# Converting float64 weights a whole unit at a time on VectorE and ScalarE alone, with the words loaded into the unit's own place

## The chip, the cores and the metric

One core of one Trainium2 chip runs the kernel. The metric is device microseconds (us) of one execution; before the change the median of 3 runs is 819.43 us (818.68 to 821.88).

## The reference, cut to what matters

Three layers follow one another: retention over 4 x 8 heads of 576 tokens, a dense layer of 2304 tokens x 512 x 2048 with a gated activation, and eight experts of which each token takes one. The dense layer's weights come to the kernel as float64, since they are drawn as float32 and multiplied by a float64 scalar.

```python
ret = scores * Dmat[None, :, :, :]
attn_out = np.matmul(ret, v)                      # (4, 8, 576, 64) -> x: (2304, 512)
...
h = x @ w_in                                      # float64 weights, 512 x 2048
g = h * (1.0 / (1.0 + np.exp(-1.702 * h)))
x = g @ w_out                                     # float64 weights, 2048 x 512
...
expert_idx = np.argmax(logits, axis=1)
out[mask] = gate_w[mask, None] * (np.maximum(x[mask] @ w1[e], 0.0) @ w2[e])
```

## The kernel before, in words

**Units.** The dense layer's 2048 hidden columns fall into 16 units of 128 (NF1). A unit holds, for each of 128 partitions, 512 numbers of w_in and 512 of w_out, in two float32 parts: a high part that TensorE multiplies in one pass, and a low part, which is the rest. So a unit is a tile of 128 x 2 x 1024. Sixteen such places form a ring (tag "unit"); the retention stage uses seven of them first, for its own tables (`slot`, L178).

**Conversion.** The float64 words come as pairs of 32-bit words (`load_wd`, L113, by SP's queue). `convert` (L119) makes a float32 of each pair: ScalarE (ACT) takes the magnitude of the high word (L121), VectorE (DVE) clamps it (L137, a tensor_scalar), shifts and masks it (L143, a tensor_scalar), puts sign and top exponent bit back (L147, a scalar_tensor_tensor), and brings in three bits of the low word (L151, likewise). Then ACT writes the high part (L127, a CAST) and GpSimd (POOL) subtracts it to get the low part (L128). All of this is done by halves of a unit, 512 numbers a partition, so that each of these lines runs 32 times. `convert` is a generator: it yields an estimate of its cost, and `pull(us)` (L648) takes pieces out of it until `us` are used up. Retention's last 24 steps each pull 0.4, and each step of the dense layer's first two blocks pulls 2.5.

**The dense layer.** Tokens fall into six blocks of 384. Blocks 0 and 1 go through the 16 units side by side (steps g0 to g31: unit 0 for block 0, unit 0 for block 1, unit 1 for block 0, and so on), and the other four blocks follow one by one (steps g32 to g95). A step i is `layer1`, 12 matmuls into h (L374); `swish`, which is a tanh on ACT (L396), a scalar_tensor_tensor on DVE (L398), a CAST on ACT that makes the high part of g (L399), and a subtraction that makes the low part (L400: on POOL for the first three blocks, where `early` is set, on DVE after them); and two steps later `layer2`, nine matmuls into o (L385). h has two buffers, so the matmuls of step i+2 wait until L398 of step i has read h. Every engine takes its instructions in the order in which this code issues them.

**Around it.** Retention's step (bp, ch) is a chunk of one pair of heads; 16 pairs (bp) of 5 chunks each. Tables and inputs of pair bp+3 are loaded at the end of pair bp, into three sets of buffers (kz, at). The same SP queue issues the words of the weights: four half units at pairs 3, 4, 7 and 9 (WD_AT, L43), the others from within `convert`, two units ahead of their use; these wait for their staging buffers (tags "stg" and "tab"). It also writes back the retention's result for blocks 2 to 5 (x0d, L314).

The functions that the change touches:

Of the kernel before, what the change touches and what calls it, by code (L numbers as in the profile page):

```python
# [10 lines left out]
F32 = mybir.dt.float32  # L11
F32R = mybir.dt.float32r
BF16 = mybir.dt.bfloat16
I32 = mybir.dt.int32
AF = mybir.ActivationFunctionType
ALU = mybir.AluOpType

P = 128
# [7 lines left out]
NF1 = F1 // P  # L26
# [13 lines left out]
WARM = 34  # L40
HOLD = NF1 - LAG - 1 - KD
STOP = 1000.0
WD_AT = (3, 4, 7, 9)  # L43
CLAMP_HI = float(np.array(0x47EFFFFF, np.int32).view(np.float32))


# [13 lines left out]
def retention_moe_kernel(  # L60
# [40 lines left out]

    units = {}

    def new_unit(u):
        units[u] = pool.tile([P, 2, 1024], F32R, tag="unit", bufs=NF1, name=f"unit{u}")
        return units[u]

    stg = {}

    ca = pool.tile([P, 4, 512], I32, tag="tab", bufs=2, name="ca")  # L110
    cs = pool.tile([P, 2, 1024], I32, tag="tab", bufs=2, name="cs")

    def load_wd(i):  # L113
        u, h = divmod(i, 2)
        t = cs[:, h, :] if u % 2 else pool.tile([P, 1024], I32, tag="stg", bufs=2, name=f"wd{i}")
        stg["d", i] = t.rearrange("p (n two) -> p n two", two=2)
        SP.dma_start(t, wd[u, :, 512 * h : 512 * (h + 1)].bitcast(I32))

    def convert():  # L119
        def magnitude(i):  # L120
            ACT.activation(ca[:, i % 4, :].bitcast(F32), stg["d", i][:, :, 1].bitcast(F32), AF.Abs)  # L121

        def split(i):
            u, h = divmod(i, 2)
            f = ca[:, i % 4, :].bitcast(F32)
            hi, lo = (units[u][:, k, 512 * h : 512 * (h + 1)] for k in range(2))
            ACT.copy(hi, f)  # L127
            POOL.tensor_tensor(lo, f, hi.bitcast(F32), ALU.subtract)  # L128

        for i in range(2):  # L130
            magnitude(i)
        for u in range(NF1):
            new_unit(u)
            halves = [2 * u, 2 * u + 1]
            for i in halves:
                a = ca[:, i % 4, :].bitcast(F32)
                DVE.tensor_scalar(a, a, 2.0**-15, CLAMP_HI, ALU.max, ALU.min)  # L137
                if u:
                    split(i - 2)
                yield 0.35  # L140
            for i in halves:
                a = ca[:, i % 4, :]
                DVE.tensor_scalar(a, a, 3, 0x3FFFFFF8, ALU.logical_shift_left, ALU.bitwise_and)  # L143
                yield 0.35
            for i in halves:
                a = ca[:, i % 4, :]
                DVE.scalar_tensor_tensor(a, stg["d", i][:, :, 1], -0x40000000, a, ALU.bitwise_and, ALU.bitwise_or)  # L147
                yield 0.61
            for i in halves:
                a = ca[:, i % 4, :]  # L150
                DVE.scalar_tensor_tensor(a, stg.pop(("d", i))[:, :, 0], 29, a, ALU.logical_shift_right, ALU.bitwise_or)  # L151
                if u + 2 < NF1:
                    load_wd(i + 4)
                if u + 1 < NF1:
                    magnitude(i + 2)
                yield 0.61
        for i in halves:
            split(i)
            yield 0.1

    def load_we(u):
        t = pool.tile([P, 1024], F32, tag="stg", bufs=2, name=f"we{u}")
# [13 lines left out]
    st = {}  # L176

    def slot(name):  # L178
        return pool.tile([P, 2048], F32, tag="unit", bufs=NF1, name=name)

    def attention():
        psum = tc.tile_pool(name="psum_a", bufs=1, space=bass.MemoryType.PSUM, reuse_waits="tile")
# [206 lines left out]
    def swish(h, name, early=False, kept=None):  # L389
        th = pool.tile([P, TB], F32, tag="th", bufs=2, name=f"{name}t")  # L390
        if kept:
            hi, lo = kept
        else:
            hi = pool.tile([P, TB], F32R, tag="g", bufs=6, name=f"{name}h")
            lo = pool.tile([P, TB], F32R, tag="g", bufs=6, name=f"{name}l")
        ACT.activation(th, h, AF.Tanh, scale=0.851)  # L396
        g = th if early else h
        DVE.scalar_tensor_tensor(g, th, 1.0, h, ALU.add, ALU.mult)  # L398
        ACT.copy(hi, g)  # L399
        (POOL if early else DVE).tensor_tensor(lo, g, hi.bitcast(F32), ALU.subtract)  # L400
        return hi, lo

    def relu(h, name):
# [205 lines left out]
    def overflow_expert(e):  # L609
# [4 lines left out]
        DVE.scalar_tensor_tensor(ids, sel, -BIG, big, ALU.mult, ALU.add)  # L614
        w = []
        for k in range(NF2 // 2):
            t = pool.tile([P, 2, 1024], F32, tag="unit", bufs=NF1, name=f"vw{e}_{k}")
            for j in range(2):
                SP.dma_start(t[:, j, :], we[NF2 * e + 2 * k + j])
                w.append(t[:, j, :])  # L620
# [27 lines left out]
    def pull(us):  # L648

        k = 0  # L650
        us += debt.pop()
        while us > 0 and k < len(bg):
            cost = next(bg[k], None)
            if cost is None:
                bg.pop(k)
            elif cost == STOP:
                k += 1
                us -= 0.7
            else:
                us -= cost  # L660
        debt.append(min(us, 0.0))

    bg.append(convert())
    for i, _ in enumerate(attention()):
        if i > 55:
            pull(0.4)
    psum = ctx.enter_context(tc.tile_pool(name="psum", bufs=1, space=bass.MemoryType.PSUM, reuse_waits="tile"))

    def fill_slots():
# [140 lines left out]
    for i in range(nd - 1):  # L810
        blk, f = steps[i]
        dense1(i)
        if blk < 2:
            pull(2.5)
            if f > 3:
                next(fill, None)
            if (blk, f) == (1, NF1 - 3):
# [148 lines left out]
```

## Time and profile before

| | |
|---|---|
| median of 3 runs | 819.43 us (818.68 to 821.88) |
| the profiled execution | 821.95 us, span 820.2 us |
| busy, share of the span | PE 93%, DVE 56%, ACT 41%, POOL 39% |
| 105 to 212 us of the span | DVE 102.68 of 107.00 us busy, PE 94.90 |
| instructions, DVE / ACT / POOL | 982 / 700 / 292 |

The profile is of one execution. PE is TensorE, PEld its weight loads, SPq the queue that issues transfers. Busy time of PE is modelled and can hide that it is not at its peak. A row of the instruction list has the start in us of the span, the duration in us, the engine, the line of the code, the operation and its tiles (out<-in), and in brackets how long the engine sat idle before it and what ended that. A row with x2 or x12 stands for that many instructions, and its duration runs from the first one's start to the last one's end. The profiled execution was 2.52 us above the median of the runs.

### The profile page before, as it was taken

The page shows a single profiled execution, that of the slowest core. Times are in us where ns is not written, and L with a number is a line of the kernel's source. Part 1 is how long each engine was busy: PE and PEld are TensorE (multiplying, and loading weights), DVE is VectorE, ACT ScalarE, POOL GpSimd, SP SyncE. Part 2 cuts the span into 40 slices and gives each one's busy share as a digit, 9 for nine tenths or more (in the row PEclk, how much of TensorE's full clock was granted, in tenths as well). Part 3 has the DMA queues.
Part 4 walks back from the last instruction along what each step waited for, and adds up shares of the span by engine and source line. Part 5 has one row for each costly group of instructions (what it writes and reads, how often), then busy time and mean ns, then how long its engine had stood idle before and what let it go on. Part 6 is the DMA issues. An engine that isn't in the chain of part 4 may idle for free.

```text
span 820.2 us, 13383 instructions
## 1 busy us (share of the span) xinstructions
PE 765.9 (93%) x4996; PEld 674.2 (82%) x4996; DVE 462.6 (56%) x982; ACT 337.8 (41%) x700; POOL 319.8 (39%) x292
## 2 busy tenths in 40 slices
PE   7786798889999999999999998999999999999995
PEld 6666687777898989898999997888888888888884
DVE  4443789999414978774475388573434434354310
ACT  3665744444345332332332333334535434444321
POOL 3433566666623453111011122333545545454311
PEclk9998999999999999999999999999999999999998
DMA  8788833568601021203000333434536646456200
GB/s 275 239 287 261 254 131 119 161 180 256 222 1 40 2 65 52 78 1 103 14 0 21 109 103 103 148 116 149 173 142 178 184 135 192 143 182 190 79 30 34
DMA packets 37130, 105.64 MB, mean 129 GB/s; under 512 B 5439, under 2 KB 8895, under 8 KB 36800
## 3 DMA queue, kind: packets, MB, share of 16 engines
q1 hardware_dynamic: 33824, 95.24, 36.8%
q0 software_dynamic: 3232, 9.46, 3.1%
q8 instruction: 41, 0.67, 0.3%
q14 instruction: 33, 0.27, 0.1%
HBM read 81.55 MB, written 24.18 MB: 129 GB/s over the span
## 4 chain that ended last, share of the span: by engine, by line
PE 49%; issue 6%; DVE 5%; POOL 2%; ACT 1%; DMA 1%; POOLq 0%; ACTq 0%
PE eo L385 12%; PE o L385 12%; PE eh L374 12%; PE h L374 11%; DVE dj L468 2%; PE tp L573 1%; DMA we<-we 1%; DVE unit L170 1%; POOL out L412 1%; POOL unit L171 1%; DVE h L398 1%; ACT unit L169 0%; PE tp L743 0%; PE dots L482 0%; PE tp L748 0%
## 5 line engine op out<-in xcount | busy, mean ns | idle before, releaser
L374 PE MATMUL h<-x,unit 128*128 128x384 f32 x1152 | 219.3, 338 | 14.3 <-DVE x_k L400 2.5
L374 PEld LDWEIGHTS h<-x,unit 128*128 128x128 f32 x1152 | 202.6, 188 | 29.6 <-DVE x_k L400 3.8
L171 POOL TENSOR_TENSOR unit<-we,unit 128x512 fp32r<-128x512 f32 x64 | 105.0, 1649 | 149.3 <-ACT unit L169 144.7
L374 PE MATMUL eh<-xt,unit 128*128 128x352 f32 x672 | 117.1, 323 | 0.0
L374 PEld LDWEIGHTS eh<-xt,unit 128*128 128x128 f32 x672 | 111.0, 188 | 6.3
L468 DVE CUSTOM_DVE_ANT_0 dj<-xr,en 128x512 f32<-128x512 f32 x120 | 101.2, 896 | 2.2 <-ACT xr L452 2.2
L170 DVE TENSOR_TENSOR unit<-we,unit 128x512 fp32r<-128x512 f32 x64 | 58.4, 912 | 43.3 <-ACT unit L169 43.3
L169 ACT CAST unit<-we 128x1024 fp32r<-128x1024 f32 x64 | 66.8, 1046 | 9.1 <-DMA we<-we 9.1
L271 ACT ACTIVATE at<-kv,tb 64x64 f32<-64x64 f32 x128 | 39.5, 308 | 28.5 <-PE kv L268 19.7
L128 POOL TENSOR_TENSOR unit<-ca,unit 128x512 fp32r<-128x512 f32 x32 | 47.5, 1501 | 4.1 <-ACT unit L127 3.9
L240 DVE TENSOR_TENSOR pr<-sc,tb 128x256 f32<-128x256 f32 x64 | 26.7, 422 | 34.7 <-PE sc L239 31.8
L239 PE MATMUL sc<-at,kz 128*64 128x128 f32 (+1 forms) x512 | 36.0, 262 | 10.3 <-DMA at<-att 8.7
L412 POOL DMA_INDIRECT out<-y,idx x24 | 23.6, 983 | 49.2 <-ACT y L582 45.3
L239 PEld LDWEIGHTS sc<-at,kz 128*64 128x64 f32 x512 | 29.9, 148 | 11.4 <-issue 5.4
L252 POOL TENSOR_TENSOR kz<-at,tb 128x512 f32<-128x512 f32 x15 | 15.6, 1042 | 58.6 <-DMA at<-att 42.0
L268 PE MATMUL kv<-at,kz 128*64 128x64 f32 x256 | 21.8, 248 | 14.2 <-ACT at L271 12.4
L268 PEld LDWEIGHTS kv<-at,kz 128*64 128x64 f32 x256 | 13.7, 142 | 25.1 <-ACT at L271 22.9
L412 POOL DMA_INDIRECT xs<-xr,slot x18 | 19.1, 1061 | 27.6 <-DVE ov_all L547 23.6
L143 DVE TENSOR_SCALAR ca<-ca 128x512 int32<-128x512 int32 x32 | 28.2, 910 | 0.0
L289 PE MATMUL ao<-pr,at 128*64 128x128 f32 x256 | 26.6, 284 | 0.0
L367 POOL TENSOR_TENSOR x<-x0s,x 128x768 fp32r<-128x768 f32 x3 | 6.3, 2086 | 49.8 <-ACT x L366 49.8
L137 DVE TENSOR_SCALAR ca<-ca 128x512 f32<-128x512 f32 x32 | 22.8, 730 | 3.2 <-ACT ca L121 3.1
(1266 smaller groups left out, 1566.9 us busy)
## 6 DMA issues: line engine op xcount, KB each, us to landing
we<-we SPq DMA_DIRECT2D x64, 512.0 KB, 3.4
at<-att SPq DMA_DIRECT2D x15, 864.0 KB, 5.5
wd<-wd SPq DMA_DIRECT2D x16, 512.0 KB, 3.8
cs<-wd SPq DMA_DIRECT2D x16, 512.0 KB, 5.1
xs<-fill SPq DMA_DIRECT2D x22, 257.0 KB, 5.5
xrow<-xr SPq DMA_DIRECT2D x18, 257.0 KB, 5.1
kz<-kt SPq DMA_DIRECT2D x32, 144.0 KB, 4.0
rin<-xs SPq DMA_DIRECT2D x8, 514.0 KB, 4.4
```

Of the source, the lines that this page charges most:

```text
L128: POOL.tensor_tensor(lo, f, hi.bitcast(F32), ALU.subtract)
L143: DVE.tensor_scalar(a, a, 3, 0x3FFFFFF8, ALU.logical_shift_left, ALU.bitwise_and)
L169: ACT.copy(w[:, 0, :], t)
L170: DVE.tensor_tensor(w[:, 1, :512], t[:, :512], w[:, 0, :512].bitcast(F32), ALU.subtract)
L171: POOL.tensor_tensor(w[:, 1, 512:], t[:, 512:], w[:, 0, 512:].bitcast(F32), ALU.subtract)
L239: PE.matmul(sc[64 * i : 64 * i + 64, j, q0:], z[:, k0 : k0 + 64], t[:, AQ + P * ch + q0 : AQ + P * (ch + 1)], start=True, stop=True)
L268: PE.matmul(kv[r], z[:, 2 * S + P * ch + 64 * j : 2 * S + P * ch + 64 * j + 64], t[:, AV + P * ch + 64 * j : AV + P * ch + 64 * j + 64], s ...
L271: ACT.activation(sbd[(NCH * bp + ch) % 3][r, r], kv[r], AF.Copy, scale=tb[r, pair, TDW + P + 2 * NCH + ch : TDW + P + 2 * NCH + ch + 1])
L374: PE.matmul(h, w[:, a, P * dc : P * (dc + 1)], xt[:, b, dc, :n], start=k == 0, stop=k == len(terms) - 1)
L385: PE.matmul(o, a[:, c0 : c0 + n], w[:, b, 512:], start=first and k == 0, stop=last and k == 2)
L412: i = POOL.indirect_dma_start(out=dst[:, :], out_offset=bass.IndirectOffsetOnAxis(ap=rows, axis=0), in_=src, in_offset=None, bounds_check= ...
L468: DVE.tensor_tensor_reduce(junk, r[:, :D], en[e // 4][:, e % 4, :], 1.0, 0.0, ALU.mult, ALU.add, dots[:, E * k + e : E * k + e + 1])
```

## The change

Each conversion step now takes a whole unit, 1024 numbers a partition. The words of unit u are loaded by one transfer of 1 MB into the place in the ring that unit u itself will take; the working copy (`words`, two buffers) has the staging buffers. The place is now a fixed number, HELD + u modulo 16. Words are loaded three units ahead: units 0, 1 and 2 at retention's pairs 4, 7 and 10, unit u+3 when the last word operation of unit u has been issued. The low part of a unit is subtracted on DVE, after the second operation of the next unit. Also the low part of g is subtracted on DVE for all blocks. Retention's last 24 steps pull 0.5, and the steps of blocks 0 and 1 pull 3.1. The lines of the changed kernel are up to four lower than those before: its L126 is the magnitude, L134 and L136 the two tensor_scalar, L142 and L146 the two scalar_tensor_tensor, L150 ACT's CAST, L129 the low part of the unit, L392, L394, L395 and L396 the four parts of swish.

```diff
-WD_AT = (3, 4, 7, 9)
+WD_AT = (4, 7, 10)
+NWD = len(WD_AT)
+HELD = 7
...
+    def unit_tile(name, shape, dt, s):
+        return pool.tile(shape, dt, tag=f"unit{s % NF1}", bufs=1, name=name)
+
     def new_unit(u):
-        units[u] = pool.tile([P, 2, 1024], F32R, tag="unit", bufs=NF1, name=f"unit{u}")
+        units[u] = unit_tile(f"unit{u}", [P, 2, 1024], F32R, HELD + u)
         return units[u]
...
-    def load_wd(i):
-        u, h = divmod(i, 2)
-        t = cs[:, h, :] if u % 2 else pool.tile([P, 1024], I32, tag="stg", bufs=2, name=f"wd{i}")
-        stg["d", i] = t.rearrange("p (n two) -> p n two", two=2)
-        SP.dma_start(t, wd[u, :, 512 * h : 512 * (h + 1)].bitcast(I32))
+    def load_wd(u):
+        t = unit_tile(f"wd{u}", [P, 2048], I32, HELD + u)
+        stg["d", u] = t.rearrange("p (n two) -> p n two", two=2)
+        SP.dma_start(t, wd[u].bitcast(I32))
...
+        words = [pool.tile([P, 1024], I32, tag="stg", bufs=2, name=f"ca{k}") for k in range(2)]
+
+        def magnitude(u):
+            ACT.activation(words[u % 2].bitcast(F32), stg["d", u][:, :, 1].bitcast(F32), AF.Abs)
+
+        def low(u):
+            DVE.tensor_tensor(units[u][:, 1, :], words[u % 2].bitcast(F32), units[u][:, 0, :].bitcast(F32), ALU.subtract)
+
+        magnitude(0)
         for u in range(NF1):
+            a = words[u % 2]
+            DVE.tensor_scalar(a.bitcast(F32), a.bitcast(F32), 2.0**-15, CLAMP_HI, ALU.max, ALU.min)
+            yield 0.67
+            DVE.tensor_scalar(a, a, 3, 0x3FFFFFF8, ALU.logical_shift_left, ALU.bitwise_and)
+            yield 0.67
+            if u:
+                low(u - 1)
+                yield 1.22
+            d = stg.pop(("d", u))
+            DVE.scalar_tensor_tensor(a, d[:, :, 1], -0x40000000, a, ALU.bitwise_and, ALU.bitwise_or)
+            if u + 1 < NF1:
+                magnitude(u + 1)
+            yield 1.22
+            DVE.scalar_tensor_tensor(a, d[:, :, 0], 29, a, ALU.logical_shift_right, ALU.bitwise_or)
+            if u + NWD < NF1:
+                load_wd(u + NWD)
             new_unit(u)
...
+            ACT.copy(units[u][:, 0, :], a.bitcast(F32))
+            yield 1.22
+        low(u)
+        yield 0.1
...
-        (POOL if early else DVE).tensor_tensor(lo, g, hi.bitcast(F32), ALU.subtract)
+        DVE.tensor_tensor(lo, g, hi.bitcast(F32), ALU.subtract)
...
         if i > 55:
-            pull(0.4)
+            pull(0.5)
...
         if blk < 2:
-            pull(2.5)
+            pull(3.1)
```

What this does to the order of instructions is shown at three places. The first is DVE from step g6 to step g8 of the dense layer. Before, ca is the working copy and wd or cs the words:

```order
L398 SCALAR_TENSOR_TENSOR g6t<-g6t,h_1690 128x384
L147 SCALAR_TENSOR_TENSOR ca<-wd_1590,ca 128x512
L151 SCALAR_TENSOR_TENSOR ca<-wd_1586,ca 128x512
L151 SCALAR_TENSOR_TENSOR ca<-wd_1590,ca 128x512
L137 TENSOR_SCALAR ca<-ca 128x512
L398 SCALAR_TENSOR_TENSOR g7t<-g7t,h_1732 128x384
L137 TENSOR_SCALAR ca<-ca 128x512
L143 TENSOR_SCALAR ca<-ca 128x512 x2
L147 SCALAR_TENSOR_TENSOR ca<-cs,ca 128x512 x2
L151 SCALAR_TENSOR_TENSOR ca<-cs,ca 128x512
L398 SCALAR_TENSOR_TENSOR g8t<-g8t,h_1771 128x384
```

And DVE with the change, at the same steps:

```order
L394 SCALAR_TENSOR_TENSOR g6t<-g6t,h_1637 128x384
L396 TENSOR_TENSOR g6l<-g6t,g6h 128x384
L142 SCALAR_TENSOR_TENSOR ca_1076<-wd_1488,ca_1076 128x1024
L146 SCALAR_TENSOR_TENSOR ca_1076<-wd_1488,ca_1076 128x1024
L394 SCALAR_TENSOR_TENSOR g7t<-g7t,h_1673 128x384
L396 TENSOR_TENSOR g7l<-g7t,g7h 128x384
L134 TENSOR_SCALAR ca_1077<-ca_1077 128x1024
L136 TENSOR_SCALAR ca_1077<-ca_1077 128x1024
L129 TENSOR_TENSOR unit_1662<-ca_1076,unit_1662 128x1024
L142 SCALAR_TENSOR_TENSOR ca_1077<-wd_1550,ca_1077 128x1024
L394 SCALAR_TENSOR_TENSOR g8t<-g8t,h_1707 128x384
```

Two subtractions that were POOL's, L396 and L129, now stand among DVE's, and the operations of one unit follow one another without another half between them. The second place is ACT at the same steps, before:

```order
L399 CAST g6h<-g6t 128x384
L121 ACTIVATE ca<-cs 128x512 x2
L127 CAST unit_1671<-ca 128x512
L396 ACTIVATE g7t<-h_1732 128x384
L399 CAST g7h<-g7t 128x384
L127 CAST unit_1671<-ca 128x512
L121 ACTIVATE ca<-wd_1712 128x512
L396 ACTIVATE g8t<-h_1771 128x384
```

and with the change:

```order
L395 CAST g6h<-g6t 128x384
L126 ACTIVATE ca_1077<-wd_1550 128x1024
L150 CAST unit_1662<-ca_1076 128x1024
L392 ACTIVATE g7t<-h_1673 128x384
L395 CAST g7h<-g7t 128x384
L126 ACTIVATE ca_1076<-wd_1621 128x1024
L392 ACTIVATE g8t<-h_1707 128x384
```

The CAST of a whole unit (L150) now stands right ahead of the tanh of a step (L392), and it needs the operation L146 that stands right ahead of that step's L394 on DVE. The third place is SP's queue between the inputs of pairs 9 and 10 (at and kz), before:

```order
L198 DMA at_86<-att 128x1728
L117 DMA cs<-wd 128x1024
L314 DMA x0d_62<-xf_786 128x384
L196 DMA kz_84<-kt 64x576 x2
L198 DMA at_87<-att 128x1728
```

and with the change:

```order
L194 DMA at_84<-att 128x1728
L119 DMA wd_769<-wd 128x2048
L310 DMA x0d_62<-xf_783 128x384
L192 DMA kz_82<-kt 64x576 x2
L194 DMA at_85<-att 128x1728
```

A transfer of 1 MB (wd, 128x2048 words) stands ahead of the inputs of pair 10 where half of it stood. The next one, unit 2, is issued behind the inputs of pair 12, where before a half was issued behind those of pair 11; the one after it, unit 3, stands behind the inputs of pair 14, where before a half stood. PE's order is the same in both kernels.

## Rows read from the trace of the kernel before

**Rows 1.** The page: the span.
```profile
span 820.2 us, 13383 instructions
```

**Rows 2.** Windows: the stretch, busy us by engine, clock, DMA share, GB/s.
```profile
60.00:105.00 45.00, 32.83 (x588) 27.78 (x586) 26.32 (x55) 28.49 (x86) 20.58 (x22) 0.92 0.79 252
105.00:212.00 107.00, 94.90 (x457) 80.57 (x457) 102.68 (x129) 49.59 (x99) 70.34 (x50) 1.00 0.55 170
```

**Rows 3.** The chain that ended last: start, us, what.
```profile
340.46 2.08 PE o L385 x9
342.54 2.10 PE h L374 x12
```

**Rows 4.** The line L398: durations in ns, then first and last start.
```profile
L398 DVE SCALAR_TENSOR_TENSOR g11t<-g11t,h x1: 541/541/541, 164.2 to 164.2; 128x384 f32<-128x384 f32 x1
```

**Rows 5.** Instructions in order of time, DVE, 204 to 222 us.
```profile
203.99 0.54 DVE L398 SCALAR_TENSOR_TENSOR g19t<-g19t,h 128x384 f32<-128x384 f32 x1
204.45 0.75 DVE L137 TENSOR_SCALAR ca<-ca 128x512 f32<-128x512 f32 x2
205.12 0.75 DVE L143 TENSOR_SCALAR ca<-ca 128x512 int32<-128x512 int32 x2
...
206.54 0.55 DVE L398 SCALAR_TENSOR_TENSOR g20t<-g20t,h 128x384 f32<-128x384 f32 x1
...
221.24 0.55 DVE L398 SCALAR_TENSOR_TENSOR g24t<-g24t,h 128x384 f32<-128x384 f32 x1 [3.63 <-ACT g24t L396]
```

**Rows 6.** Groups by line and shape: busy us, mean ns, idle before.
```profile
L143 DVE TENSOR_SCALAR ca<-ca 128x512 int32<-128x512 int32 x32 | 28.2, 910 | 0.0
```

**Rows 7.** Instructions in order of time, POOL, 118 to 124 us.
```profile
119.83 2.90 POOL L128 TENSOR_TENSOR unit<-ca,unit 128x512 fp32r<-128x512 f32 x2
```

**Rows 8.** Instructions in order of time, DVE, 118 to 125 us.
```profile
120.08 2.94 DVE L143 TENSOR_SCALAR ca<-ca 128x512 int32<-128x512 int32 x2
122.94 0.68 DVE L147 SCALAR_TENSOR_TENSOR ca<-wd,ca 128x512 int32<-128x512 int32 x1
123.54 0.54 DVE L398 SCALAR_TENSOR_TENSOR g3t<-g3t,h 128x384 f32<-128x384 f32 x1
```

**Rows 9.** Instructions in order of time, DVE, 345 to 347 us (block 3).
```profile
345.27 0.56 DVE L398 SCALAR_TENSOR_TENSOR h<-g53t,h 128x384 f32<-128x384 f32 x1 [0.56 <-ACT g53t L396]
346.38 0.56 DVE L400 TENSOR_TENSOR g53l<-h,g53h 128x384 fp32r<-128x384 f32 x1 [0.55 <-ACT g53h L399]
346.85 0.69 DVE L468 CUSTOM_DVE_ANT_0 dj<-xr,en 128x512 f32<-128x512 f32 x1
```

**Rows 10.** Instructions in order of time, ACT, 200 to 207 us.
```profile
200.31 1.23 ACT L121 ACTIVATE ca<-cs 128x512 f32<-128x512 f32 x2
201.46 0.47 ACT L396 ACTIVATE g19t<-h 128x384 f32<-128x384 f32 x1
...
204.98 1.14 ACT L127 CAST unit<-ca 128x512 fp32r<-128x512 f32 x2
206.02 0.48 ACT L396 ACTIVATE g20t<-h 128x384 f32<-128x384 f32 x1
```

**Rows 11.** Instructions in order of time, PE in retention, with their waits.
```profile
65.33 0.56 PE L239 MATMUL sc<-at,kz 128*64 128x128 f32 x8 [2.79 <-DMA at<-att]
...
78.86 0.56 PE L239 MATMUL sc<-at,kz 128*64 128x128 f32 x8 [2.52 <-DMA at<-att]
```

**Rows 12.** Instructions in order of time, PE at pair 15.
```profile
97.88 0.56 PE L239 MATMUL sc<-at,kz 128*64 128x128 f32 x8 [2.21 <-DMA at<-att]
```

**Rows 13.** Instructions in order of time, SP's queue: transfers issued.
```profile
52.17 0.42 SPq L117 DMA_DIRECT2D cs<-wd  x1
...
56.91 0.51 SPq L198 DMA_DIRECT2D at<-att  x1
...
65.21 0.34 SPq L117 DMA_DIRECT2D cs<-wd  x1
```

**Rows 14.** Instructions in order of time, PE in block 2.
```profile
293.87 0.17 PE L515 MATMUL rk<-oh_all,ub 128*128 128x24 bf16 x1 [1.71 <-DVE dots L468]
```

More of the change, by code (lines that the diff above doesn't have):

```diff
@@ L102, in retention_moe_kernel @@
     units = {}
+    def unit_tile(name, shape, dt, s):
+        return pool.tile(shape, dt, tag=f"unit{s % NF1}", bufs=1, name=name)
     def new_unit(u):
-        units[u] = pool.tile([P, 2, 1024], F32R, tag="unit", bufs=NF1, name=f"unit{u}")
+        units[u] = unit_tile(f"unit{u}", [P, 2, 1024], F32R, HELD + u)
         return units[u]
     stg = {}
-    ca = pool.tile([P, 4, 512], I32, tag="tab", bufs=2, name="ca")
-    cs = pool.tile([P, 2, 1024], I32, tag="tab", bufs=2, name="cs")
-    def load_wd(i):
-        u, h = divmod(i, 2)
-        t = cs[:, h, :] if u % 2 else pool.tile([P, 1024], I32, tag="stg", bufs=2, name=f"wd{i}")
-        stg["d", i] = t.rearrange("p (n two) -> p n two", two=2)
-        SP.dma_start(t, wd[u, :, 512 * h : 512 * (h + 1)].bitcast(I32))
@@ L119, in convert @@
-    def convert():
[L120 to L131, printed above, removed]
-        for u in range(NF1):
-            new_unit(u)
[L134 to L159, printed above, removed]
@@ L178, in slot @@
     def slot(name):
-        return pool.tile([P, 2048], F32, tag="unit", bufs=NF1, name=name)
+        st["slots"] = st.get("slots", -1) + 1
+        assert st["slots"] < HELD
+        return unit_tile(name, [P, 2048], F32, st["slots"])
     def attention():
@@ L616, in overflow_expert @@
         for k in range(NF2 // 2):
-            t = pool.tile([P, 2, 1024], F32, tag="unit", bufs=NF1, name=f"vw{e}_{k}")
+            t = unit_tile(f"vw{e}_{k}", [P, 2, 1024], F32, k)
             for j in range(2):
```

## The prediction

> **What bounds the kernel now.** I read the windows first, then the chain of waits, then the instructions in order of time on the engine that the chain blames. The profiled execution took 821.95 us, of which the span is 820.2 us [rows 1]. In a dense step without waiting PE works 2.10 us on the 12 matmuls into h and 2.08 us on the nine into o, so 4.18 us a step [rows 3]. One stretch is far from that: from 105 to 212 us DVE is busy for 102.68 of 107.00 us, PE for 94.90 [rows 2]. That is where the weights are converted. There the step's scalar_tensor_tensor on DVE, which frees h, starts at 123.54 us for g3, 164.2 us for g11 and 203.99 us for g19 [rows 4, 5, 8]: 40.7 and 39.8 us for eight steps, **5.03 us a step**. DVE sets the pace there. By g24, at 221.24 us, the conversion is over and PE sets it [rows 5].
>
> Why DVE is so slow there is seen at 120 us. Two tensor_scalar take 2.94 us while two of POOL's subtractions run, which take 2.90 us [rows 7, 8]; with POOL idle the same pair is started and followed within 0.67 us [rows 5]. So POOL's work costs DVE time, and over the kernel the 32 of L143 alone took 28.2 us, 910 ns each [rows 6], where 0.67/2 x 32 is 10.7 us.
>
> **The change part by part.** With POOL's subtractions gone from this stretch, DVE runs at the undisturbed rate. I price a whole unit's operations from undisturbed halves. A scalar_tensor_tensor over 512 is followed 0.60 us after its start [rows 8], one over 384 after 0.46 us [rows 5]. That is 1.0 to 1.1 ns a number (the rows are rounded) and some 0.06 us for the start, which a whole saves once: 1.14 us over 1024 (bounds 1.09 and 1.20). A tensor_scalar is 0.67 us for two halves [rows 5], so 0.61 us (bounds 0.56 and 0.67). No row has the subtraction over 1024; like the scalar_tensor_tensor it reads two tensors, so I take 1.14 us for it as well. A unit is then 2 x 0.61 + 3 x 1.14 = 4.64 us of DVE.
>
> The Trainium skill, page "SBUF — State Buffer", section "Who interferes with whom", says that a VectorE instruction with two SBUF inputs, or in a two-port mode, and a GpSimd instruction that reads SBUF exclude one another for the whole instruction. The trace agrees for the tensor_scalar [rows 7, 8]. By that rule alone the conversion would be all gain, the first rival below.
>
> The subtraction of g's low part comes on top. In block 3, where it already is DVE's, scalar_tensor_tensor, wait for ACT's CAST and subtraction together take DVE from 345.27 to 346.85 us: 1.58 us a step, of which 0.55 us is idle [rows 9]. Before, DVE spent 0.46 us a step on this [rows 5]. The pattern of the order repeats after eight steps: 8 x 3.1 of pull against 2 x 0.67 + 3 x 1.22 = 5.0 a unit is five units. So DVE's own sum for eight steps is 5 x 4.64 + 8 x 1.58 = **35.8 us**, 4.48 us a step. That is less than 5.03, but already more than PE's 4.18.
>
> Now the wait that the order adds. ACT's CAST of a whole unit stands right ahead of a step's tanh, and it needs the last word operation on DVE. Behind that operation DVE has the step's scalar_tensor_tensor, which needs the tanh. So DVE stands idle for CAST and tanh together, although h has long been ready, and PE waits behind it. A CAST of two halves takes ACT 1.04 us from start to the next start [rows 10]; I take 1.0 us for a whole. The magnitude takes 1.15 us for two halves [rows 10]; I take 1.1 us. From the tanh's start to DVE's it is 0.52 us (206.02 to 206.54 us) [rows 5, 10]. Counted over the eight steps g2 to g9 of the changed order, what stands ahead of the step's scalar_tensor_tensor on DVE is
>
> - the last word operation, twice: 1.0 + 0.52 = 1.52 us idle each, 3.0 us;
> - the first tensor_scalar of the next unit, once: 1.52 - 0.61 = 0.9 us;
> - the second tensor_scalar, once: 1.52 - 1.22 = 0.3 us;
> - the sign operation, twice: the next unit's magnitude starts with it, so 1.1 + 0.52 - 1.14 = 0.5 us each, 1.0 us;
> - the unit's subtraction, twice: nothing.
>
> Together 5.2 us. Also, an operation that needs the result of the one right before it can't start in its tail, which is 0.08 us (0.68 us long, followed after 0.60 us) [rows 8]; eight such places make 0.6 us. So eight steps take 35.8 + 5.2 + 0.6 = 41.6 us: **5.2 us a step**, against 5.03 before. And conversion now lasts until g22 in the order.
>
> From g3, which I leave at 123.5 us, to g22 are 19 steps: 123.5 + 19 x 5.2 = 222.3 us. g22 frees h 0.55 us later, PE then needs 2.10 us for the matmuls of g24, and the tanh 0.52 us: g24 on DVE at 225.5 us, where it was 221.24 us [rows 5]. **The dense stretch loses 4.3 us.** After that PE sets the pace as before, so nothing gives them back. Bounds: without the idle time 4.48 us a step and a gain of 9.4 us (the first rival); with the upper prices of all operations about 5.4 us a step and a loss of 8 us.
>
> Retention pulls its inputs through a busy SP queue. The DMA share there is 0.79 at 252 GB/s [rows 2], and PE waits at three places for inputs that came late: 2.79, 2.52 and 2.21 us [rows 11, 12]. Half a unit is 0.52 MB: 1.6 us at a full share (252/0.79 = 319 GB/s), 2.1 us at 252. Unit 1 now puts 1 MB ahead of pair 10's inputs, where half of it was issued at 52.17 us, before the inputs at 56.91 us that came at 65.33 us [rows 11, 13]: + 1.6 to 2.1 us on the first wait. The half at 65.21 us [rows 13] no longer stands ahead of pair 12's inputs: as much less on the second. Unit 3 stands ahead of pair 15's with 1 MB where half stood: 0 to + 2.1 us. I take + 1.0 us in all, between - 2.2 us (the third wait goes, since no load waits for its staging buffer any longer) and + 4.2 us. Retention's DVE has room for its part of the conversion (26.32 of 45.00 us) [rows 2]: nothing.
>
> In block 2 the low part of g moves onto DVE beside the routing. There PE waited once, 1.71 us [rows 14], on DVE's dot products. These are no longer held up by POOL, but each step has 1.1 us more in front of them. I take nothing, bounds - 1.7 and + 1.5 us. The other edits (places in the ring, names) issue nothing.
>
> Sum: 4.3 + 1.0 + 0 = + 5.3 us, 827.3 us on the profiled execution. That one lay 2.52 us above the median of the runs shown, so against the median: 819.43 + 5.3 = **824.7 us**.
>
> **Rivals.** *VectorE freed and ACT in time: faster.* If the tanh were ready when DVE comes to it, eight steps would be DVE's own 35.8 us, g22 would be at 123.5 + 19 x 4.48 = 208.6 us, and g24 at 211.8 us: 9.4 us earlier, with + 1.0 us in retention 811.0 us. For it: POOL's price in rows 6 to 8 is real and goes. Against it: the order printed above puts the CAST ahead of the tanh. It decides as soon as the idle time falls below 2 us in eight steps. The rule of the Trainium skill on the shared ports, taken alone, gives this time.
>
> *The words flood retention's queue: slower still.* If the DMA share is full from 50 to 100 us, units 1, 2 and 3 delay inputs by 2.1 us each and nothing is given back: + 6.3 us there in place of + 1.0, 830.0 us. For it: three late inputs already. Against it: a mean share of 0.79 leaves 9 of the 45 us free.
>
> *Both prices cancel: no change.* With half of the idle time (2.6 us) a step takes 4.88 us; g24 comes 1.8 us earlier, and with + 1.0 us the time is 818.6 us.
>
> **How the numbers follow.** A measurement of this kernel can tell about 0.5%, 4.1 us, from no change: below 815.3 us is faster, above 823.5 us slower. The forecast has 0.60; its own range is 820 to 829 us, of which I count 0.38 as slower and 0.22 as within. The faster rival has 0.17, the flood 0.14 (slower), the balance 0.09 (within). So faster 0.17, within 0.31, slower 0.52. The range leaves out half of the faster rival and the upper part of the flood: 812 to 831 us.
>
> **What would show it.** Right: in the changed profile DVE's whole operations last about 1.2 us (0.7 us the tensor_scalar) with POOL idle; before the steps' scalar_tensor_tensor DVE sits idle for up to 1.5 us, ended by ACT's tanh, with a CAST of a whole unit just before that on ACT; eight steps take about 41.6 us; PE waits longer than before on the step's scalar_tensor_tensor; g24 comes near 225 us. Wrong: steps of 4.5 us or less from g3 on, or a PE that waits for inputs in retention 4 us more or less than the 7.5 us of rows 11 and 12.

## The result and the profile after

The change is slower: 827.73 us, the median of six runs (826.13 to 829.83), against 819.05 us for the kernel before on the same chip (six runs, 816.51 to 821.88). The ratio is 1.0104, with a 95% interval of 1.0084 to 1.0125. The profiled execution of the change took 827.56 us.

The page of the changed kernel: the span, and the busy time of each engine.

```profile
span 825.8 us, 13185 instructions
PE 769.6 (93%) x4996; PEld 677.9 (82%) x4996; DVE 451.0 (55%) x982; ACT 336.0 (41%) x668; POOL 214.2 (26%) x212
```

POOL lost 80 instructions, and PE is as busy as it was. So the loss must be looked for by stage. The windows of [rows 2], now of the changed kernel:

```profile
60.00:105.00 45.00, 34.89 (x608) 28.85 (x605) 26.02 (x48) 29.90 (x85) 20.77 (x22) 0.96 0.79 274
105.00:212.00 107.00, 91.95 (x433) 79.28 (x432) 81.07 (x103) 45.61 (x66) 0.00 (x0) 0.97 0.51 179
```

From 105 to 212 us POOL does nothing, and DVE went from 102.68 to 81.07 us of work. Yet PE did less, 91.95 us where it did 94.90. Nobody is full there any more: that is the mark of engines that wait for one another. DVE in order of time (start, duration, line, operation, and in brackets the idle time before it and what ended it) shows where:

```profile
138.47 1.22 DVE L142 SCALAR_TENSOR_TENSOR ca<-wd,ca 128x1024 int32<-128x1024 int32 x1
139.73 1.23 DVE L146 SCALAR_TENSOR_TENSOR ca<-wd,ca 128x1024 int32<-128x1024 int32 x1
142.45 0.56 DVE L394 SCALAR_TENSOR_TENSOR g7t<-g7t,h 128x384 f32<-128x384 f32 x1 [1.50 <-ACT g7t L392]
143.59 0.56 DVE L396 TENSOR_TENSOR g7l<-g7t,g7h 128x384 fp32r<-128x384 f32 x1 [0.58 <-ACT g7h L395]
144.06 0.69 DVE L134 TENSOR_SCALAR ca<-ca 128x1024 f32<-128x1024 f32 x1
144.79 0.69 DVE L136 TENSOR_SCALAR ca<-ca 128x1024 int32<-128x1024 int32 x1
145.40 1.22 DVE L129 TENSOR_TENSOR unit<-ca,unit 128x1024 fp32r<-128x1024 f32 x1
146.53 1.22 DVE L142 SCALAR_TENSOR_TENSOR ca<-wd,ca 128x1024 int32<-128x1024 int32 x1
148.27 0.56 DVE L394 SCALAR_TENSOR_TENSOR g8t<-g8t,h 128x384 f32<-128x384 f32 x1 [0.52 <-ACT g8t L392]
...
152.60 0.55 DVE L394 SCALAR_TENSOR_TENSOR g9t<-g9t,h 128x384 f32<-128x384 f32 x1 [0.17 <-ACT g9t L392]
```

And ACT at the same steps:

```profile
140.99 1.05 ACT L150 CAST unit<-ca 128x1024 fp32r<-128x1024 f32 x1 [1.96 <-DVE ca L146]
141.94 0.48 ACT L392 ACTIVATE g7t<-h 128x384 f32<-128x384 f32 x1
...
146.69 1.17 ACT L126 ACTIVATE ca<-wd 128x1024 f32<-128x1024 f32 x1 [3.14 <-DVE unit L129]
147.74 0.50 ACT L392 ACTIVATE g8t<-h 128x384 f32<-128x384 f32 x1
```

Read the two together. DVE's L146 ends at 140.96 us, and only then can ACT begin the CAST of the unit (140.99). The tanh of g7 stands behind that CAST and starts at 141.94, and DVE's next instruction needs the tanh: 1.50 us of idle time on the engine that has the most to do. PE pays for it. Its waits from 105 to 320 us, grouped (what it waited for, us in all, times, the longest); before, the longest in this stretch was rk's 1.71 us [rows 14]:

```profile
PE rk L511 <- DVE dots L464: 2.5, 1, 2.5
PE h L370 <- DVE g10t L394: 2.3, 1, 2.3
PE h L370 <- DVE g18t L394: 2.3, 1, 2.3
PE h L370 <- DVE g2t L394: 1.8, 1, 1.8
PE h L370 <- DVE g8t L394: 1.4, 1, 1.4
```

The chain of waits is no help here. For the stretch from retention to block 2 it holds one piece:

```profile
101.56 146.91 issue
```

So the loss is best read from landmarks, the starts of the tanh of g0, g31 and g48 on ACT. The kernel before and the change were each profiled a second time, with unchanged code, and the table has both executions of each (us, from the span's start):

| | before | before, again | change | change, again |
|---|---|---|---|---|
| start to tanh of g0 (retention) | 107.26 | 103.57 | 105.32 | 104.92 |
| tanh of g0 to g31 (blocks 0 and 1) | 144.08 | 144.12 | 149.53 | 149.55 |
| tanh of g31 to g48 (block 2) | 72.27 | 72.27 | 74.45 | 74.60 |
| the execution | 821.95 | 818.65 | 827.56 | 827.64 |

Blocks 0 and 1 lost 5.4 us and block 2 lost 2.2 to 2.3 us, and both figures repeat to 0.2 us. Retention doesn't repeat: one code gives 107.3 and 103.6 us. What lies behind g48 took 496.5 to 496.8 us in all four.

### The profile page after: what moved, and what is told of

It is laid out like the page before. It is cut to its first block, busy times and chain, and to the rows that moved or that the text cites. A ratio compares the mean times of both kernels' runs of the same rounds, so it can differ in the third digit from the quotient of the medians.

```text
span 825.8 us, 13185 instructions
## 1 busy us (share of the span) xinstructions
PE 769.6 (93%) x4996; PEld 677.9 (82%) x4996; DVE 451.0 (55%) x982; ACT 336.0 (41%) x668; POOL 214.2 (26%) x212
## 4 chain that ended last, share of the span: by engine, by line
PE 59%; issue 24%; DVE 6%; DMA 4%; ACT 4%; POOL 2%; SPq 0%; POOLq 0%; ACTq 0%; DVEq 0%
PE o L381 14%; PE h L370 13%; PE eo L381 13%; PE eh L370 12%; DMA at<-att 3%; DVE dj L464 2%; ACT at L267 1%; PE kv L264 1%; PE sc L235 1%; DMA kz<-kt 1%; PE tp L569 1%; DVE unit L164 1%; PE ao L285 1%; PE ao L282 1%; POOL out L408 1%
## 5 line engine op out<-in xcount | busy, mean ns | idle before, releaser
L464 DVE CUSTOM_DVE_ANT_0 dj<-xr,en 128x512 f32<-128x512 f32 x120 | 92.8, 827 | 1.1 <-ACT xr L448 1.0
L431 POOL TENSOR_TENSOR enrm<-scr,c 128x8 f32<-128x8 f32 x1 | 1.7, 1688 | 146.9 <-ACT ej L436 146.9
L150 ACT CAST unit<-ca 128x1024 fp32r<-128x1024 f32 x16 | 16.8, 1050 | 24.7 <-DVE ca L146 24.6
L126 ACT ACTIVATE ca<-wd 128x1024 f32<-128x1024 f32 x16 | 18.6, 1160 | 16.6 <-DVE unit L129 16.5
```

Source lines behind the costliest of these rows:

```text
L464: DVE.tensor_tensor_reduce(junk, r[:, :D], en[e // 4][:, e % 4, :], 1.0, 0.0, ALU.mult, ALU.add, dots[:, E * k + e : E * k + e + 1])
```

## The experiments

Four ideas were to be told apart. *Order*: the loss comes from the CAST of a whole unit ahead of a tanh. *Pace*: too much conversion is handed to each step, whatever its order. *Routing*: block 2 loses since the low part of g delays the dot products of the routing on DVE. *Work*: DVE has simply been given too much. Ratios are to the kernel before on the same chip. Differences in us to the change are to its 827.73 us above; the medians of the kernel before beside these runs lie between 818.92 and 820.83 us (819.05 us above), so such a difference can be off by up to 2 us.

**Less conversion beside each step.** The change, with one number different:

```diff
-            pull(3.1)
+            pull(2.6)
```

> The changed kernel with pull(2.6) in place of pull(3.1) in the steps of blocks 0 and 1; the same instructions, spread over some 26 steps in place of 22. Theory 'pace' (the loss is that conversion is packed into 22 steps, each of which DVE can't finish in PE's 4.18 us, while the steps behind them leave DVE idle): eight steps take 39 to 40 us in place of 42.4, block 1 ends about 7 us earlier, 820 to 822 us. Theory 'place' (the loss is the DVE idle time ahead of each step's scalar_tensor_tensor, which depends on what stands there and not on the pace): idle time per conversion step the same, and little gain, 826 to 828 us.

Measured: 820.33 us, 0.9996 (0.9978 to 1.0013), in the 820 to 822 us that pace expected. The whole loss is gone, 7.4 us, although the idle time is not: DVE's waits for the tanh, from 118 to 234 us, grouped, some of them, in this kernel:

```profile
DVE g14t L394 <- ACT g14t L392: 1.6, 1, 1.6
DVE g8t L394 <- ACT g8t L392: 1.5, 1, 1.5
DVE g12t L394 <- ACT g12t L392: 1.5, 1, 1.5
...
DVE g20t L394 <- ACT g20t L392: 0.9, 1, 0.9
```

Over the 26 steps that now have conversion beside them (g1 to g26) they add up to 15.8 us, in the change to 12.9 us over 22 steps (g1 to g22). But spread over more steps, they and the work fit better under PE's time for a step: from 105 to 212 us PE is busy for 97.22 us where it was 91.95.

**The CAST after the tanh.** The change with its pieces in another order: the CAST of unit u-1 behind the second operation of unit u, the subtraction behind the sign operation, the magnitude last.

```diff
+            if u:
+                high(u - 1)
             yield 0.67
+            d = stg.pop(("d", u))
+            DVE.scalar_tensor_tensor(a, d[:, :, 1], ...)
+            yield 1.22
             if u:
                 low(u - 1)
                 yield 1.22
-            d = stg.pop(("d", u))
-            DVE.scalar_tensor_tensor(a, d[:, :, 1], ...)
-            if u + 1 < NF1:
-                magnitude(u + 1)
-            yield 1.22
...
-            ACT.copy(units[u][:, 0, :], a.bitcast(F32))
+            if u + 1 < NF1:
+                magnitude(u + 1)
```

> The changed kernel with ACT's CAST of a unit issued after the second tensor_scalar of the next unit, the unit's subtraction after the next unit's sign operation, and the magnitude after the last word operation; pull stays 3.1, the same instructions. Theory 'order' (DVE waits for tanh behind the whole-unit CAST on ACT): the waits of about 1.5 us ahead of the scalar_tensor_tensor go, DVE's idle time there falls from about 15 us to about 5 us, eight steps take 38 to 39 us in place of 42.4, 817 to 819 us. Theory 'work' (the two subtractions on DVE are simply too much work): eight steps stay above 41 us, 826 to 829 us.

Measured: 819.87 us, 0.9992 (0.9971 to 1.0013). The same operations at the same pace, 7.9 us less; 817 to 819 us were expected of order. (`high` is ACT's CAST of a unit.) On ACT the tanh now goes first, and the CAST follows the step's own (in order of time):

```profile
163.36 0.50 ACT L397 ACTIVATE g12t<-h 128x384 f32<-128x384 f32 x1
164.71 0.51 ACT L400 CAST g12h<-g12t 128x384 fp32r<-128x384 f32 x1 [0.85 <-DVE g12t L399]
165.13 1.05 ACT L132 CAST unit<-ca 128x1024 fp32r<-128x1024 f32 x1
```

and DVE's scalar_tensor_tensor of that step (its L399) starts at 164.13 us with no idle time before it. Over g1 to g22 DVE's idle time before these operations is 3.1 us, where the change has 12.9. From the tanh of g8 to that of g16 it takes 38.6 us, where the change takes 42.5. Order and pace are each enough to take the loss back. Both do it in blocks 0 and 1, which take 142.1 us with the pull of 2.6 and 140.1 us with the late CAST, less than the 144.1 us before the change; block 2 keeps its loss (74.4 and 74.8 us).

**Block 2's low part of g on POOL.** The change, with POOL for that block alone:

```diff
-        DVE.tensor_tensor(lo, g, hi.bitcast(F32), ALU.subtract)
+        (POOL if early == 2 else DVE).tensor_tensor(lo, g, hi.bitcast(F32), ALU.subtract)
...
-        gs[blk, f] = swish(h, f"g{i}", blk < 3, ...)
+        gs[blk, f] = swish(h, f"g{i}", 2 if blk == 2 else blk < 2, ...)
```

> The changed kernel with the low part of g back on POOL for block 2 alone (blocks 0 and 1 stay on DVE). Theory 'routing' (the longer wait of PE before the rk matmuls, 2.54 us after against 1.71 us before, and the lower clock behind it, come from the 1.1 us a step that the low part of g adds to DVE in block 2): the wait is 1.7 us or less, no drop of the clock, about 2 us faster than the change, 825.5 us. Rival (POOL's work delays the dot products by as much): no change, 827 to 829 us.

Measured: 825.52 us, 1.0072 (1.0045 to 1.0098), 2.2 us less than the change, and block 2 takes 72.19 us, as it did before the change (72.27). The wait of PE on the dot products, in the change and then in this kernel:

```profile
298.13 0.18 PE L511 MATMUL rk<-oh_all,ub 128*128 128x24 bf16 x1 [2.54 <-DVE dots L464]
```

```profile
295.63 0.17 PE L511 MATMUL rk<-oh_all,ub 128*128 128x24 bf16 x1 [1.70 <-DVE dots L464]
```

It is 0.84 us shorter, less than the 2.2 us. The rest stands in the clock: the windows behind that wait (the last three columns are the granted clock, the DMA share and GB/s), again of the change and then of this kernel:

```profile
298.00:300.00 2.00, 1.87 (x8) 1.57 (x8) 1.42 (x6) 0.52 (x1) 0.63 (x3) 0.50 0.00 0
300.00:302.00 2.00, 2.00 (x7) 1.53 (x7) 1.93 (x6) 0.00 (x0) 0.00 (x0) 0.66 0.00 0
302.00:304.00 2.00, 2.00 (x13) 2.00 (x13) 0.14 (x2) 0.00 (x0) 0.00 (x0) 1.00 0.00 0
```

```profile
295.00:297.00 2.00, 1.37 (x10) 1.15 (x10) 2.00 (x5) 0.81 (x3) 1.38 (x1) 1.00 0.00 0
297.00:299.00 2.00, 2.00 (x12) 1.83 (x11) 1.93 (x6) 0.51 (x1) 0.92 (x1) 1.00 0.00 0
```

After the wait of 2.54 us the granted clock is 0.50, the level of 1.2 GHz, and 0.66 on average in the next 2 us. After 1.70 us it stays at 1.00. In the slow 4 us the engine gets through 15 matmuls, where this kernel gets through 22 in the 4 us from 295 us, the end of its wait included.

**The words one pair later, before the change.** The place of the last half in retention's queue, moved on its own in the kernel before:

```diff
-WD_AT = (3, 4, 7, 9)
+WD_AT = (3, 4, 7, 10)
```

> The kernel before with its fourth half unit loaded at pair 10 in place of pair 9. After the change the dense layer starts 2 us earlier than before. Theory 'place of the loads' (the half unit at pair 9 stood ahead of pair 12's inputs): the wait of 2.52 us at 78.9 us goes, the dense layer starts 1.5 to 2 us earlier, 817 to 818 us. Rival (it is the loads that wait for a staging buffer, or POOL's subtractions in retention): the dense layer starts at about 104.8 us as before, 819 us.

Measured: 819.94 us, 0.9997 (0.9976 to 1.0018): no gain, so the theory's 817 to 818 us missed. In its profile the tanh of g0 came 2.45 us earlier than in [rows 1]'s execution, but in the second profile of the unchanged kernel it came 3.7 us earlier. A gain in a stage that scatters so much can't be read from one profile. Blocks 0 and 1 then took 145.6 us, where the kernel before took 144.1; why is not shown.

**Less conversion beside each step, before the change.** If pace is what counts, the old kernel must have the same lever:

```diff
-            pull(2.5)
+            pull(2.0)
```

> The kernel before with pull(2.0) in place of pull(2.5) in the steps of blocks 0 and 1: its conversion is spread over some 26 steps in place of 21. Theory 'pace': a unit's DVE work of about 7.2 us (halves, POOL beside it) comes to 0.52 units, 3.8 us, a step, and 4.2 us with the step's own 0.47 us, so PE nearly sets the pace: from g0 to g31 132 to 136 us in place of 144.1, 808 to 812 us. Rival 'POOL' (it is POOL's interference as such that holds PE, whatever the pace): about 144 us and 819 us again.

Measured: 803.52 us, 0.9789 (0.9757 to 0.982), 24.2 us under the change. The gain is larger than either theory expected: from g0 to g31 it takes 128.5 us, where 132 to 136 us were expected. The window:

```profile
105.00:212.00 107.00, 106.08 (x535) 95.89 (x534) 103.85 (x129) 51.64 (x103) 71.40 (x53) 1.00 0.51 168
```

DVE is as busy as in [rows 2] (103.85 us), and POOL holds it up no less than before: the 32 of L143 have a median of 1144 ns here and of 626 ns in the kernel before. Yet PE works 106.08 of 107 us. The amount put into each step is what held the kernel before back here: with less of it, neither POOL's interference nor DVE's high busy share had to go. What the interference costs at a pull of 2.5 this run doesn't show.

**The low part of g back on POOL.** The change, with that one part undone for blocks 0 to 2:

```diff
-        DVE.tensor_tensor(lo, g, hi.bitcast(F32), ALU.subtract)
+        (POOL if early else DVE).tensor_tensor(lo, g, hi.bitcast(F32), ALU.subtract)
```

> The changed kernel with the low part of g back on POOL for blocks 0, 1 and 2 (as before); the units' low parts stay on DVE. It undoes one part. Theory 'order and work': DVE loses 1.1 us of work and idle time a step and keeps the waits behind ACT's CAST; eight steps come to some 33 us without POOL's interference and some 40 us if POOL's 1.2 to 1.5 us a step block DVE in full: 811 to 823 us, faster than the change. Rival (POOL's interference is worth more than the subtraction costs DVE): 828 us or more.

Measured: 817.61 us, 0.9966 (0.9952 to 0.9979), 10.1 us less than the change. Each step loses the subtraction and the wait for ACT's CAST in front of it (0.58 us at g7l above). The waits of 1.50 us are still there, and POOL's interference is back. DVE, then POOL, in order of time:

```profile
138.61 0.55 DVE L394 SCALAR_TENSOR_TENSOR g7t<-g7t,h 128x384 f32<-128x384 f32 x1 [1.50 <-ACT g7t L392]
139.08 0.69 DVE L134 TENSOR_SCALAR ca<-ca 128x1024 f32<-128x1024 f32 x1
139.80 1.55 DVE L136 TENSOR_SCALAR ca<-ca 128x1024 int32<-128x1024 int32 x1
```

```profile
139.79 1.02 POOL L396 TENSOR_TENSOR g7l<-g7t,g7h 128x384 fp32r<-128x384 f32 x1 [3.77 <-ACT g7h L395]
```

The 0.86 us that L136 loses (1.55 against 0.69) is less than the 1.1 us that the step saves. So work counts too: with less of it on DVE the loss goes, with the pace and the waits of 1.50 us left as they were.

**The unit's low part on POOL.** The other half of the removed GpSimd work, given back alone:

```diff
-            DVE.tensor_tensor(units[u][:, 1, :], ...)
+            POOL.tensor_tensor(units[u][:, 1, :], ...)
```

> The low half of a whole unit is subtracted on GpSimd, all else as in the change. If VectorE's amount of work sets the pace, its 1.2 us of every unit leave it, some 5 to 6 us in eight steps, and the time comes down to 815 to 820. If the order of the two queues sets it, the unit's sign op only waits for a slower subtraction on GpSimd, the idle time ahead of the dense stage's scalar_tensor_tensor stays, GpSimd's subtraction stretches VectorE's ops beside it, and the time stays at 823 to 830.

Measured: 822.98 us, 1.0057 (1.004 to 1.0074), between the two ranges expected. The idle time stays (four waits of 1.5 us from g7 to g18), as order said; but eight steps, from the tanh of g8 to that of g16, take 39.9 us in place of 42.5. That is less than the 5.7 us of the five subtractions, because of rows like these, POOL and then DVE:

```profile
150.59 2.41 POOL L129 TENSOR_TENSOR unit<-ca,unit 128x1024 fp32r<-128x1024 f32 x1 [5.85 <-ACT unit L150]
```

```profile
150.93 0.56 DVE L394 SCALAR_TENSOR_TENSOR g9t<-g9t,h 128x384 f32<-128x384 f32 x1 [0.18 <-ACT g9t L392]
152.06 1.35 DVE L396 TENSOR_TENSOR g9l<-g9t,g9h 128x384 fp32r<-128x384 f32 x1 [0.58 <-ACT g9h L395]
```

Beside POOL's operation (150.59 to 153.00 us) DVE's subtraction takes 1.35 us, where alone it takes 0.56. L394, which reads one tensor out of SBUF and h out of PSUM, is not touched.

**Both remedies together, and the routing too.** First the late CAST with a pull of 2.5, then that with POOL for block 2's low part of g; the edits are those above.

> The changed kernel with both edits at once: ACT's CAST and the unit's subtraction later (as in the run with the late CAST) and pull(2.5). If order and pace are both causes and add up, DVE needs about 2.5 us of conversion (0.5 units of 4.6 us, 2.3 us), 1.6 us of swish and little idle time a step, just under PE's 4.18 us: from g0 to g31 129 to 132 us in place of 149.5, 808 to 810 us. If one edit makes the other useless: 817 to 820 us as for each of them alone.

Measured: 808.21 us, 0.9849 (0.9819 to 0.9879). PE is busy for 106.88 of the 107 us from 105 to 212 us. Order and pace add up, as expected: from g0 to g31 it takes 127.5 us, 22.0 us less than the change, where the pull of 2.6 alone gave 7.5 and the late CAST alone 9.4.

> The run before, and the low part of g of block 2 on POOL. The longer wait before rk is a separate cause, so it adds up: another 2 us faster, 806 to 808 us, the wait before rk 1.7 us and no drop of the clock there. If DVE is no longer late when it comes to block 2, the wait is short anyway: no difference from the run before.

Measured: 803.39 us, 0.9801 (0.977 to 0.9833), the same as the kernel before at its own better pace (803.52). Both beat the two kernels of the comparison. The 4.8 us between this run's median and that of the run before are more than the 2 us expected. In their two profiles, 8.1 us apart, block 2 has 0.7 us of the difference (73.0 and 72.3 us, with PE's wait before rk at 1.70 us here) and retention, whose code is the same in both, has 5.7 us (108.2 and 102.5). So most of the distance is not the routing's.

**How far pace goes.** The change in its own order at 2.3:

```diff
-            pull(3.1)
+            pull(2.3)
```

> The change with 2.3 instead of 3.1 of conversion beside each step, its order otherwise left alone (the whole CAST still ahead of a tanh). If pace alone decides, the idle time is covered like the rest: DVE's own work a step falls to some 4.0 us (1.58 for the step, 2.3 of conversion by the code's prices) under PE's 4.18, and the time is that of the late CAST at 2.5, 806 to 811. If a single 1.5 us of idle time still reaches PE because it falls into one step (4.0 + 1.5 is over 4.18), the steps that hold it stay long and the time is 812 to 818.

Measured: 822.5 us, 1.0026 (1.0002 to 1.0049), outside both ranges expected. A new wait shows, PE from 105 to 330 us, grouped:

```profile
PE h L370 <- DVE unit L129: 9.8, 9, 2.6
```

and in order of time, a few of the nine:

```profile
153.07 2.03 PE L370 MATMUL h<-x,unit 128*128 128x384 f32 x10 [0.40 <-DVE unit L129]
...
190.47 2.02 PE L370 MATMUL h<-x,unit 128*128 128x384 f32 x10 [1.02 <-DVE unit L129]
...
211.39 3.57 PE L370 MATMUL h<-x,unit 128*128 128x384 f32 x10 [2.65 <-DVE unit L129]
```

At 2.3 the units come out too late for the steps that multiply by them. At 2.6 in this order, and at 2.5 with the late CAST, nobody waits for a unit. So the pace has a bound on either side. At 211.39 us the ten matmuls take 3.57 us in place of 2.03, at a granted clock of 0.50 (212 to 216 us): part of the loss is the clock behind such a wait.

**The second profiles.** The two kernels of the comparison, unchanged:

> The kernel before, unchanged, profiled a second time, for the 2 us by which the retention stage (first instruction to the tanh of g0) was shorter in the one profile of the change (105.3 against 107.3 us). If single executions of one code scatter there, this one gives another figure than 107.3 by 1 us or more, and 105.3 lies within what the kernel before does by itself. If the change really shortens the stage, it stays at 107.3 within 0.5 us. From the dense stage on (tanh of g0 to tanh of g31) both expect 144.1 within 0.5 us.

> The change, unchanged, profiled a second time. Scatter: the retention stage takes anything from 103 to 108 us. A real gain of the change: 105.3 within 0.5 us. From the dense stage on, both expect 149.5 within 0.5 us, and block 2 (tanh of g31 to tanh of g48) 74.4 against 72.3 before, with the wait of rk's matmul near 2.5 us.

Measured: the table above. Retention of one code scatters by 3.7 us, so the scatter holds for the kernel before; the two executions of the change happened to lie 0.4 us apart.

## Why the prediction was right

The forecast was 824.7 us, in a range of 820 to 829 us, and 827.73 us were measured: + 8.7 us where + 5.3 was said.

**DVE's own amount and the idle time.** The forecast counted 5.2 us of idle time in eight steps, and the trace has 5.2 (g7 to g14: 1.50, 0.52, 0.17, 1.50, 0, 0.95, 0.53 and 0). That is no luck: over g2 to g9, the steps that it counted, the trace has 1.50, 0, 0.90, 0.52, 0, 1.50, 0.52 and 0.17 us, each within 0.15 us of what the prediction's list gives for the operation that stands there. Eight steps were to take 41.6 us and took 42.5, the scalar_tensor_tensor of g11 and of g19 in the list of that line:

```profile
L394 DVE SCALAR_TENSOR_TENSOR g11t<-g11t,h x1: 547/547/547, 163.4 to 163.4; 128x384 f32<-128x384 f32 x1
...
L394 DVE SCALAR_TENSOR_TENSOR g19t<-g19t,h x1: 547/547/547, 205.9 to 205.9; 128x384 f32<-128x384 f32 x1
...
L394 DVE SCALAR_TENSOR_TENSOR g24t<-g24t,h x1: 555/555/555, 224.7 to 224.7; 128x384 f32<-128x384 f32 x1
```

The 0.9 us lies in the main in DVE's own work: the part of a step outside the conversion took 1.61 us (142.45 to 144.06) where 1.58 was taken, and a word operation that needs the one before it 1.26 us (138.47 to 139.73) where 1.14 + 0.08 = 1.22 was. From g3, at 121.0 us, to g22, at 221.1 us, it came to 100.1 us where nineteen steps of 5.2 make 98.8; g24 stands at 224.7 us (225.5 in the forecast), but from a g3 that started 2.6 us earlier. From g3 to g24, the stretch that the forecast counted, it is 103.7 us where it was 97.7 before, so + 6.0 us; ahead of g3 the change gave 0.6 us back, which the forecast did not have. So the **dense term was + 5.4 us where + 4.3 was said**. The late CAST takes the dense loss back with the same operations and with 9.7 us less idle time, so the wait named in the prediction is a cause of it. It is one only at this pace and this amount of work: the runs at 2.6 and with the low part of g on POOL take the loss back with the waits of 1.50 us in place.

What the prediction didn't see is how much depends on pace. It took the conversion's end at g22 as given and worked out what each step would cost. The runs at 2.6 and, before the change, at 2.0 show that the same work spread over more steps costs much less, since a step that fits under PE's 4.18 us adds nothing to PE's time.

**Retention.** Taken at + 1.0, bounds - 2.2 and + 4.2. No pair of profiles can show it: the two profiles of the kernel before differ by 3.7 us. By subtraction, 8.7 us between the medians less 5.4 and 2.2 leaves 1.1 us; the interval of the ratio (6.9 to 10.2 us) leaves - 0.7 to + 2.6. That this lies close to + 1.0 is no support for the term. Six executions ran the change's code for retention (the change twice, the pulls of 2.6 and 2.3, and the two runs with low parts of g on POOL) and took 103.7 to 105.3 us up to the tanh of g0, 104.5 us in the mean; three ran that of the kernel before (twice unchanged, and the pull of 2.0) and took 103.6 to 107.3 us, 105.5 in the mean. So no profile shows a loss there. The waits for inputs sum to 5.0 and 5.6 us in the two profiles of the change, against 7.5 in [rows 11, 12] and 3.4 in the second profile of the kernel before. So the sign that the prediction named, 4 us more or less than 7.5 us of such waits, could not have told anything: the kernel before differs by 4.1 us from itself. This term stays open, as does which transfer is late.

**Block 2.** Taken at 0, bounds - 1.7 and + 1.5, **and this is the mis-sized term: + 2.2 us**, above its upper bound. The dot products were not sooner for want of POOL; each step's 1.1 us more on DVE in front of them made rk wait 2.54 us instead of 1.71 [rows 14]. The upper bound had the wait and not the clock behind it, which the run with POOL in block 2 takes away along with the wait.

**The rivals.** ACT in time (811.0 us) fell by the rows of 1.50 us. Even with the CAST behind the tanh, which takes most of these waits away, eight steps take 38.6 us, above the 35.8 us that the rival took, and the time is 819.87 us, no better than before. The balance (818.6) fell with the same rows. The flood (830.0) has no support: the waits for inputs are no longer than in the first profile before. The sum of the prediction, 5.3 us, was low by 1.1 us in the dense stage and 2.2 us in block 2. That is the distance to the 8.7 us of the medians only if retention's + 1.0 is left as it is, and this no run shows.

The rule of the Trainium skill that the prediction weighed (page "SBUF — State Buffer", section "Who interferes with whom") is that a VectorE instruction with two SBUF inputs and a GpSimd instruction that reads SBUF exclude one another. It agrees with the rows above (0.56 us alone and 1.35 us beside POOL with two inputs from SBUF, no effect on L394). The first rival took from it alone that taking GpSimd away is all gain; here what that gives back is lost again when the work goes to the engine that sets the pace.

## What to carry to other kernels

Background work in an in-order queue is a rate, and the rate has to be set against the step of the engine that should be the bound: too fast, and each step grows past it; too slow, and the results come too late. Here one number was worth some 17 us before the change (820.21 to 803.52 us on one chip) and some 7 us after it. An operation made twice as large should also be looked at from the other engine's queue, for what then stands behind it.

A stage that scatters between executions of one code should be profiled twice before its gain is believed, and stages that repeat to 0.1 us should carry the argument.

## What the runs showed that was not expected

**The clock after a wait.** Of the profiles here, the seven in which PE waited 2.5 to 2.8 us for the dot products in block 2 (the change twice, and the runs with pulls of 2.6 and 2.3, the late CAST, the unit's low part on POOL, and the late CAST at 2.5) include six in which the granted clock then fell to 0.50 for 2 to 4 us. In the seven with waits of 1.7 us it stayed at 1.00. Among the long waits the exception is the late CAST with a pull of 2.5, which waited 2.52 us and kept 1.00; its row and the window behind it (granted clock third from the end):

```profile
278.99 0.17 PE L516 MATMUL rk<-oh_all,ub 128*128 128x24 bf16 x1 [2.52 <-DVE dots L469]
```

```profile
279.00:281.00 2.00, 2.00 (x12) 1.67 (x12) 1.42 (x4) 0.51 (x1) 0.65 (x3) 1.00 0.00 0
```

Its block 2 took 73.0 us, where the change took 74.5 with an equal wait and the kernel before 72.3. So of the 2.2 us about 1.4 belong to the clock and 0.8 to the wait.

The length of a wait alone doesn't decide it, and neither does the code. In both profiles of the change PE waits 2.29 us before the h of g12. PE's row and a window behind it, in the first profile and then in the second:

```profile
159.93 2.97 PE L370 MATMUL h<-x,unit 128*128 128x384 f32 x12 [2.29 <-DVE g10t L394]
162.00:164.00 2.00, 2.00 (x7) 1.71 (x7) 1.94 (x3) 0.02 (x1) 0.00 (x0) 0.50 0.00 0
```

```profile
159.54 2.35 PE L370 MATMUL h<-x,unit 128*128 128x384 f32 x12 [2.29 <-DVE g10t L394]
162.00:164.00 2.00, 2.00 (x11) 1.64 (x10) 1.55 (x2) 0.41 (x1) 0.00 (x0) 1.00 0.00 0
```

The clock fell to 0.50 in the first and stayed at 1.00 in the second. What tells such waits apart is not shown. Nor did it cost anything there, where DVE sets the pace: blocks 0 and 1 took 149.5 us in both profiles, and also in the run with block 2's low part of g on POOL, which has one such fall in these blocks where the change has two.

**Interference that costs nothing.** With POOL beside it DVE's tensor_scalar took more than four times its own time before the change (2.94 us for a pair that takes 0.67 [rows 5, 8]), and at a pull of 2.0 PE still worked 106.08 of 107 us, with DVE busy for 103.85.
